# Cross network on Trainium2: the first layer as one product, its remainder rows on VectorE, and two transfers swapped

## The chip, the cores and the metric

The kernel runs on one core of one Trainium2 chip. Its time is device time in microseconds (us), the median of the runs shown. Beside it stands one profiled execution, whose own time and span are used where instructions are counted; the span is measured from the first to the last instruction, so what lies before and after it is not in it.

## The reference

Six layers of a cross network. Every layer multiplies the running activation by a square weight matrix, adds a bias, multiplies by the network's input and adds the running activation. The input is 4096 rows of 416 features, all in bf16.

```python
B, F, D, L = 4096, 26, 16, 6
Din = min(F * D, 1024)          # 416
# x0 (4096, 416), ws (6, 416, 416), bs (6, 416)
def reference(x0, ws, bs):
    x = x0
    for l in range(ws.shape[0]):
        x = x0 * (x @ ws[l] + bs[l]) + x
    return x
```

In the first layer x is x0 itself.

## The kernel before

**Layout.** Features lie on partitions. Of the 416 features, 384 make three blocks of 128 (`NK = 3`, index `m` for output blocks and `k` for input blocks) and 32 are left over, the remainder. The 4096 rows are two halves (`s = 0, 1`) of 2048, each of four column groups (`g`) of 512 columns. `XM[0]` holds the transposed x0 of the three blocks, `XM[1]` and `XM[2]` the running activation by turns; `XR[0..2]` hold the remainder, with group g of a half on partitions 32g to 32g+31. `XRx` is a copy of the first `XR` with its two partition halves exchanged.

**Loads.** The x0 blocks come in by DMA transposes, one for each column group (`load_x0t(s, g)`, line 78), all issued on SP's queue in a written order; the remainder comes as rows (`load_xrem`, line 83): half 0 in two parts (partitions 0 to 63 from ACT's queue, 64 to 127 from SP's) and half 1 in one. Behind the eight transposes SP issues the later layers' weights (`load_wm`, `load_wr`), the x0 rows for the last layer and the last bias. `x0_rem` (lines 155 to 160) turns remainder rows into `XR[0]`: a 32x32 block transpose, a reordering copy, and the copy into `XRx`. For the second part of half 0 the two copies run on GpSimd (POOL), for the others on VectorE (DVE).

**First layer.** `first_layer(s)` (line 208) fills three pairs of PSUM banks with columns groups 0 and 1 (`pa[m]`, by `full`, line 214, three matmuls for one block and group), adds the remainder's contribution (`row`, line 221), and does the same for groups 2 and 3 (`pb[m]`). PSUM has four such pairs, handed out in turn by `two_banks`, so a new block waits until ACT has emptied the pair that it takes over. `rem_first` computes the remainder's own output for both halves.

**Eviction.** `ew_main` (lines 162 to 167) empties a pair of banks: ACT adds the bias `bM` and writes bf16 into one of six buffers `t`, DVE multiplies `t` by x0 (line 166) and adds the running activation (line 167). `ew_rem` (lines 169 to 173) does this for the remainder with `bR`.

**Layers 1 to 4** go through six tiles (half s, block m) two by two: `mm_full` (line 179) and `mm_row` (line 185) for the tile, then its evictions; `rem_pair` (lines 191, 196) stands behind the first two tiles. The first tile's `mm_row` reads the remainder activation of the layer before. **The last layer** works with rows on partitions (lines 332 to 346) and writes the output.

Every engine executes its own instructions in the order in which the kernel's text issues them; the order is written out by hand, and no scheduler moves anything.

Of the kernel before, what the change touches and what calls it, by code (L numbers as in the profile page):

```python
# [10 lines left out]
ALU = mybir.AluOpType  # L11
# [5 lines left out]
def kernel(  # L17
# [7 lines left out]
    nc = tc.nc  # L25
    B, D = x0.shape
    L = ws.shape[0]
    P = 128
    NK = 3
# [4 lines left out]
    CW = 512  # L34
# [24 lines left out]
    bM = const.tile([P, NK, L], FP32)  # L59
    bR = const.tile([P, L], FP32)  # L60
# [5 lines left out]
    XRx = [big.tile([P, CW], BF16, name=f"XRx{s}") for s in range(NS)]  # L66
    XM = [big.tile([P, NK, B], BF16, name=f"XM{i}") for i in range(3)]
    XR = [big.tile([P, NS * CW], BF16, name=f"XR{i}") for i in range(3)]

    def col0(s, g):  # L70
        return SW * s + CW * g
# [4 lines left out]
    def load_x0t(s, g):  # L76
        c0 = col0(s, g)
        nc.sync.dma_start_transpose(out=XM[0][:, :, c0:c0 + CW], in_=x0[c0:c0 + CW, 0:NK * P])  # L78


    def load_xrem(eng, s, p0, p1):
        with nc.allow_non_contiguous_dma(reason="64B row segments"):
            eng.dma_start(xrem[s][p0:p1], x0[SW * s + 16 * p0:SW * s + 16 * p1, NK * P:D].rearrange("(p t) r -> p t r", t=16))  # L83
# [18 lines left out]
        nc.vector.tensor_copy(WR[32 * g:32 * g + 32, 0, :], WR[0:32, 0, :])  # L102
    load_x0t(0, 1)
    load_x0t(0, 2)
    load_xrem(nc.sync, 0, 64, 128)
    load_x0t(0, 3)
    load_x0t(1, 0)
    load_x0t(1, 1)
    load_xrem(nc.sync, 1, 0, 128)
# [21 lines left out]
    def two_banks():  # L131
        i = 2 * (turn[0] % 4)
        turn[0] += 1
        return PS[:, i:i + 2, :]

    def pe_filler(n, cols):
        for i in range(n):
            nc.tensor.matmul(PS[:, 0, 0:cols], lhsT=warm[:, 0:P], rhs=warm[:, 0:cols], start=True, stop=True, skip_group_check=True)  # L138
# [4 lines left out]
    def bias_setup():  # L143
        pb = PS[:, 7, 0:32].rearrange("p (a b) -> p a b", a=4)
        for m in range(NK):
            nc.tensor.matmul(pb[:, m, 0:L], lhsT=bsb[0:L, 128 * m:128 * m + 128], rhs=ident[0:L, 0:L], start=True, stop=True,
                             skip_group_check=True)
        for g in range(NG):
            nc.tensor.matmul(pb[32 * g:32 * g + 32, 3, 0:L], lhsT=bsb[0:L, NK * P:D], rhs=ident[0:L, 0:L], start=True, stop=True,
                             tile_position=(0, 32 * g), skip_group_check=True)  # L150
        nc.vector.tensor_copy(bM[:], pb[:, 0:NK, 0:L])
        nc.vector.tensor_copy(bR[:], pb[:, 3, 0:L])


    def x0_rem(s, p0, p1, eng):
        nc.vector.transpose(out=xrt[s][p0:p1], in_=xrem[s][p0:p1])  # L156
        eng.tensor_copy(XR[0][p0:p1, CW * s:CW * s + CW].rearrange("p (j t) -> p j t", t=16),
                              xrt[s][p0:p1].rearrange("p t j -> p j t"))
        for a in range(p0, p1, 64):
            eng.tensor_copy(XRx[s][64 - a:128 - a, :], XR[0][a:a + 64, CW * s:CW * s + CW])  # L160

    def ew_main(l, s, m, h, pt, cur, nxt):
        c0 = col0(s, 2 * h)
        t = tpool.tile([P, 2 * CW], BF16, name="t")
        nc.scalar.activation(t[:], pt.rearrange("p a b -> p (a b)"), ACT.Identity, bias=bM[:, m, l:l + 1], scale=1.0)  # L165
        nc.vector.tensor_tensor(out=t[:], in0=t[:], in1=XM[0][:, m, c0:c0 + 2 * CW], op=ALU.mult)  # L166
        nc.vector.tensor_tensor(out=nxt[:, m, c0:c0 + 2 * CW], in0=t[:], in1=cur[:, m, c0:c0 + 2 * CW], op=ALU.add)  # L167

    def ew_rem(l, s, pr, curR, nxtR):
        tr = tpool.tile([P, 2 * CW], BF16, name="t")  # L170
        nc.scalar.activation(tr[:, 0:CW], pr, ACT.Identity, bias=bR[:, l:l + 1], scale=1.0)  # L171
        nc.vector.tensor_tensor(out=tr[:, 0:CW], in0=tr[:, 0:CW], in1=XR[0][:, CW * s:CW * s + CW], op=ALU.mult)
        nc.vector.tensor_tensor(out=nxtR[:, CW * s:CW * s + CW], in0=tr[:, 0:CW], in1=curR[:, CW * s:CW * s + CW], op=ALU.add)  # L173

    def mm_full(l, s, m, g, pts, cur, first, last):
# [32 lines left out]
    def first_layer(s):  # L208
        cur, nxt = XM[0], XM[1]

        def full(pt, m, h, gl, first, last):
            c0 = col0(s, 2 * h + gl)
            for k in range(NK):
                nc.tensor.matmul(pt[:, gl, :], lhsT=WM[:, 0, k, 128 * m:128 * m + 128], rhs=cur[:, k, c0:c0 + CW],  # L214
                                 start=(first and k == 0), stop=(last and k == NK - 1), skip_group_check=True)

        def row(pt, m, h, swapped, first):
            for gl in range(2):
                r0 = 32 * ((2 * h + gl + 2 * swapped) % 4)
                src = XRx[s][r0:r0 + 32, :] if swapped else XR[0][r0:r0 + 32, CW * s:CW * s + CW]  # L220
                nc.tensor.matmul(pt[:, gl, :], lhsT=WR[r0:r0 + 32, 0, 128 * m:128 * m + 128], rhs=src,
                                 start=first, stop=(not first), tile_position=(r0, 0), skip_group_check=True)

        pa = [two_banks() for m in range(NK)]
        if s == 0:
            for gl in range(2):
                for m in range(NK):
                    full(pa[m], m, 0, gl, True, False)
        else:
            for m in range(NK):  # L230
                for gl in range(2):
                    full(pa[m], m, 0, gl, True, False)
        pb = [two_banks()]
        row(pa[0], 0, 0, 0, False)
        row(pa[1], 1, 0, 1, False)
        row(pa[2], 2, 0, 0, False)
        if s == 1:
            row(pb[0], 0, 1, 0, True)
        if s == 0:
            x0_rem(0, 64, 128, nc.gpsimd)  # L240
        for m in range(NK):
            ew_main(0, s, m, 0, pa[m], cur, nxt)
        for gl in range(2):
            full(pb[0], 0, 1, gl, s == 0, s == 1)
        if s == 1:
            ew_main(0, s, 0, 1, pb[0], cur, nxt)
        for m in range(1, NK):
            pb.append(two_banks())
            for gl in range(2):
                full(pb[m], m, 1, gl, True, False)  # L250
        if s == 0:
            row(pb[0], 0, 1, 0, False)
            row(pb[2], 2, 1, 1, False)
            row(pb[1], 1, 1, 0, False)
            x0_rem(1, 0, 128, nc.vector)
            for m in range(NK):
                ew_main(0, s, m, 1, pb[m], cur, nxt)
        else:
            row(pb[1], 1, 1, 0, False)
            row(pb[2], 2, 1, 1, False)  # L260
            rem_first(pb)

    bias_setup()
    pe_filler(1, CW)
    x0_rem(0, 0, 64, nc.vector)

    def rem_pair(l, cur, curR, nxtR, feeds_last):
        pr2 = two_banks()
        for s in range(NS):
            mm_rem(l, s, pr2[:, s, :], cur, curR)  # L270
        for s in range(NS):
            ew_rem(l, s, pr2[:, s, :], curR, nxtR)
            if feeds_last:
                nc.sync.dma_start_transpose(out=scrR[s][:], in_=nxtR[:, CW * s:CW * s + CW])
                nc.gpsimd.tensor_copy(XLrows[:, 16 * s:16 * s + 16, NK * P:D].rearrange("p (g i) r -> p i g r", g=NG),  # L275
                                      scrR[s][:].rearrange("p i (g r) -> p i g r", g=NG))

    def rem_first(pb):
        pr2 = two_banks()
        for s in range(NS):  # L280
            mm_rem(0, s, pr2[:, s, :], XM[0], XR[0])
        for s in range(NS):
            ew_rem(0, s, pr2[:, s, :], XR[0], XR[1])
            ew_main(0, 1, 1 + s, 1, pb[1 + s], XM[0], XM[1])

    first_layer(0)
    fill_wd(1, L)
    first_layer(1)
    cur, curR = XM[1], XR[1]
    for l in range(1, LL):  # L290
        nxt, nxtR = XM[1 + (l % 2)], XR[1 + (l % 2)]
# [27 lines left out]
    l = LL  # L319
# [107 lines left out]
```

## Time and profile before

| | us |
|---|---|
| median of 3 runs | 132.49 (131.76 to 132.85) |
| profiled execution, its own time | 132.9 |
| its span, first to last instruction | 131.1 |
| PE (TensorE matmul) busy | 122.8 |
| DVE busy | 111.2 |
| ACT busy | 84.0 |
| POOL busy | 8.3 |
| mean granted TensorE clock | 0.991 of full speed |

Engines work at the same time, so their busy times don't add up to the span. A row of a timeline gives the start, the duration from the first start to the last end of the merged instructions, the engine (a trailing q means the engine's queue of DMA issues), the line, the operation and the count; what stands in brackets is idle time of that engine ahead of the row and what ended it. A matmul of 512 columns has a row of 0.38 us, but one starts every 0.22 us, since matmuls are pipelined; a short stall is therefore seen in the distance between starts and not as idle time.

### The profile page before, as it was taken

How to read it: one execution, taken by the hardware profiler on the slowest of the kernel's cores; microseconds unless marked ns; L12 is line 12 of the kernel's file. 1: busy time of each engine (PE TensorE's matmuls, PEld its weight loads, DVE VectorE, ACT ScalarE, POOL GpSimd, SP SyncE). 2: the span in 40 equal slices, each digit the busy share in tenths (PEclk: the TensorE clock that was granted, in tenths of full speed). 3: DMA queues.
4: the chain of work that ended last, by engine and by line, in shares of the span. 5: the costliest groups of instructions: out<-in, count | busy, mean ns of one | idle time of the engine just before them, and what ended most of it. 6: DMA issues, size and time to landing. Idle time of an engine off the chain costs nothing.

```text
span 131.1 us, 3942 instructions
## 1 busy us (share of the span) xinstructions
PE 122.8 (94%) x1681; PEld 54.5 (42%) x1683; DVE 111.2 (85%) x196; ACT 84.0 (64%) x92; POOL 8.3 (6%) x20
## 2 busy tenths in 40 slices
PE   6996999997999999999999999999999999999950
PEld 2342343443434344544454444344544445544420
DVE  1256939999999999999898989898989999999990
ACT  1307196686939485939477948668757777567760
POOL 4105000250000000000000000000000400000000
PEclk9999999999999999999999999999999999999996
DMA  3999999999990000000000000000297899996553
GB/s 92 264 184 171 182 160 251 216 313 333 332 331 28 5 0 3 5 0 5 0 5 0 5 0 5 0 0 5 49 156 164 169 131 235 199 329 206 184 179 100
DMA packets 42021, 16.37 MB, mean 125 GB/s; under 512 B 30826, under 2 KB 42004, under 8 KB 42004
## 3 DMA queue, kind: packets, MB, share of 16 engines
q1 hardware_dynamic: 40504, 15.70, 54.5%
q10 hardware_dynamic: 1500, 0.42, 1.5%
q8 instruction: 13, 0.21, 0.7%
q14 instruction: 4, 0.03, 0.1%
HBM read 6.15 MB, written 3.41 MB: 73 GB/s over the span
## 4 chain that ended last, share of the span: by engine, by line
PE 72%; SPq 16%; DMA 5%; DVE 3%; issue 1%; ACT 0%; DVEq 0%
PE PS L179 46%; SPq L78 13%; PE PS L332 12%; PE PS L185 5%; DMA WM<-in_ws_dram 5%; PE PS L196 4%; PE PS L341 2%; SPq L86 1%; PE PS L191 1%; PE PS L346 1%; SPq L83 1%; DVE t L367 1%; SPq L74 1%; DVE o L370 1%; DVE t L166 1%
## 5 line engine op out<-in xcount | busy, mean ns | idle before, releaser
L165 ACT ACTIVATE t<-PS,bM 128x1024 bf16<-128x1024 f32 x60 | 62.2, 1115 | 32.2 <-PE PS L185 22.1
L179 PE MATMUL PS<-XM,WM 128*32 128x512 bf16 x1152 | 65.2, 379 | 0.0
L167 DVE TENSOR_TENSOR XM<-t,XM 128x1024 bf16<-128x1024 bf16 x60 | 42.2, 703 | 3.5
L166 DVE TENSOR_TENSOR t<-t,XM 128x1024 bf16<-128x1024 bf16 x60 | 42.1, 702 | 2.4 <-ACT t L165 2.4
L179 PEld LDWEIGHTS <-WM 128*32 128x32 bf16 x1152 | 29.7, 97 | 33.8 <-issue 5.1
L332 PE MATMUL PS<-WM,XM 128*128 128x416 bf16 x96 | 17.9, 340 | 0.0
L214 PE MATMUL PS<-XM,WM 128*128 128x512 bf16 x70 | 16.4, 379 | 1.4 <-DMA XM<-in_x_dram 1.2
L356 ACT CAST t<-PS 128x832 bf16<-128x832 f32 x12 | 10.2, 852 | 5.0 <-PE PS L332 2.5
L332 PEld LDWEIGHTS <-XM 128*128 128x128 bf16 x96 | 8.9, 98 | 8.7 <-issue 2.2
L214 PEld LDWEIGHTS <-WM 128*128 128x128 bf16 x72 | 6.8, 97 | 10.6 <-issue 3.2
L196 PE MATMUL PS<-XM,WM 128*32 128x512 bf16 x120 | 8.2, 379 | 0.0
L185 PE MATMUL PS<-XR,WR 32*128 32x512 bf16 x96 | 7.3, 379 | 0.7 <-DVE XR L173 0.7
L171 ACT ACTIVATE t<-PS,bR 128x512 bf16<-128x512 f32 x10 | 6.8, 695 | 1.7 <-PE PS L196 1.7
L358 DVE TENSOR_TENSOR o<-t,XLrows 128x832 bf16<-128x832 bf16 x12 | 7.1, 592 | 0.5
L357 DVE TENSOR_TENSOR t<-t,X0rows 128x832 bf16<-128x832 bf16 x12 | 7.0, 584 | 0.0
L275 POOL COPY XLrows<-scrR 128x512 bf16<-128x512 bf16 x2 | 1.4, 694 | 73.9 <-DMA scrR<-XR 73.9
L138 PE MATMUL PS<-warm 128*128 128x512 bf16 (+1 forms) x12 | 4.8, 576 | 1.2 <-DVE warm L89 1.2
L156 DVE STREAM_TRANSPOSE xrt<-xrem 64x512 bf16<-64x512 bf16 (+1 forms) x3 | 2.1, 708 | 3.8 <-DMA xrem<-in_x_dram 3.8
L173 DVE TENSOR_TENSOR XR<-t,XR 128x512 bf16<-128x512 bf16 x10 | 4.2, 425 | 0.8
L366 ACT CAST t<-PS 128x416 bf16<-128x416 f32 x8 | 4.0, 506 | 1.0 <-PE PS L332 0.8
L196 PEld LDWEIGHTS <-WM 128*32 128x32 bf16 x120 | 3.2, 97 | 3.2
L102 DVE COPY WR<-WR 32x416 bf16<-32x416 bf16 x3 | 0.8, 260 | 4.4 <-DMA WR<-in_ws_dram 4.3
(37 smaller groups left out, 40.7 us busy)
## 6 DMA issues: line engine op xcount, KB each, us to landing
X0rows<-in_x_dram SPq DMA_DIRECT2D x4, 832.0 KB, 10.0
out_dram<-o SPq DMA_DIRECT2D x12, 208.0 KB, 2.3
WM<-in_ws_dram SPq DMA_DIRECT2D x5, 312.0 KB
out_dram<-o SPq DMA_DIRECT2D x8, 104.0 KB, 1.8
WR<-in_ws_dram SPq DMA_DIRECT2D x4, 130.0 KB, 5.4
WM<-in_ws_dram ACTq DMA_DIRECT2D x1, 312.0 KB, 3.2
XM<-in_x_dram SPq DMA_TRANSPOSE x8, 4.8
xrem<-in_x_dram SPq DMA_DIRECT2D x1, 128.0 KB
```

What stands on the lines that cost most here:

```text
L78: nc.sync.dma_start_transpose(out=XM[0][:, :, c0:c0 + CW], in_=x0[c0:c0 + CW, 0:NK * P])
L165: nc.scalar.activation(t[:], pt.rearrange("p a b -> p (a b)"), ACT.Identity, bias=bM[:, m, l:l + 1], scale=1.0)
L166: nc.vector.tensor_tensor(out=t[:], in0=t[:], in1=XM[0][:, m, c0:c0 + 2 * CW], op=ALU.mult)
L167: nc.vector.tensor_tensor(out=nxt[:, m, c0:c0 + 2 * CW], in0=t[:], in1=cur[:, m, c0:c0 + 2 * CW], op=ALU.add)
L179: nc.tensor.matmul(pts[g // 2][32 * q:32 * q + 32, g % 2, :], lhsT=WM[:, l, k, 128 * m + 32 * q:128 * m + 32 * q + 32], rhs=cur[:, k, c0:c ...
L185: nc.tensor.matmul(pts[g // 2][:, g % 2, :], lhsT=WR[32 * g:32 * g + 32, l, 128 * m:128 * m + 128], rhs=curR[32 * g:32 * g + 32, CW * s:CW ...
L196: nc.tensor.matmul(pr[32 * g:32 * g + 32, :], lhsT=WM[:, l, k, NK * P:D], rhs=cur[:, k, c0:c0 + CW], start=False, stop=(k == NK - 1), tile ...
L214: nc.tensor.matmul(pt[:, gl, :], lhsT=WM[:, 0, k, 128 * m:128 * m + 128], rhs=cur[:, k, c0:c0 + CW], start=(first and k == 0), stop=(last ...
L332: nc.tensor.matmul(py[g // 2][:, g % 2, 0:D], lhsT=cur[:, k, q_cols(q, g)], rhs=WM[:, l, k, :], start=(first and k == 0), stop=((not first ...
L356: nc.scalar.copy(tv, py[h][:, :, 0:D])
L357: nc.vector.tensor_tensor(out=tv, in0=tv, in1=X0rows[:, b0:b0 + 5:4, :], op=ALU.mult)
L358: nc.vector.tensor_tensor(out=o[:], in0=tv, in1=XLrows[:, b0:b0 + 5:4, :], op=ALU.add)
```

## The change

It has four parts. The first layer's bias columns of `bM` and `bR` are stored with 1 added, and for layer 0 `ew_main` and `ew_rem` write the product of `t` and x0 straight into the next activation and return, without the add. The fourth column group's transpose of half 0 is issued ahead of the remainder's second part. The two copies of that part move from POOL to DVE. In half 1 the first blocks come in the order (m, group) (0,0), (1,0), (0,1), (1,1), (2,0), (2,1), and in half 0 the remainder rows of `pb` come in the order 0, 1, 2.

```diff
     load_x0t(0, 2)
+    load_x0t(0, 3)
     load_xrem(nc.sync, 0, 64, 128)
-    load_x0t(0, 3)
     load_x0t(1, 0)
...
-        nc.vector.tensor_copy(bM[:], pb[:, 0:NK, 0:L])
-        nc.vector.tensor_copy(bR[:], pb[:, 3, 0:L])
+        nc.vector.tensor_scalar(out=bM[:, :, 0:1], in0=pb[:, 0:NK, 0:1], scalar1=1.0, scalar2=None, op0=ALU.add)
+        nc.vector.tensor_scalar(out=bR[:, 0:1], in0=pb[:, 3, 0:1], scalar1=1.0, scalar2=None, op0=ALU.add)
+        nc.vector.tensor_copy(bM[:, :, 1:L], pb[:, 0:NK, 1:L])
+        nc.vector.tensor_copy(bR[:, 1:L], pb[:, 3, 1:L])
...
-    def x0_rem(s, p0, p1, eng):
+    def x0_rem(s, p0, p1):
...
-        eng.tensor_copy(XR[0][p0:p1, ...
+        nc.vector.tensor_copy(XR[0][p0:p1, ...
...
-            eng.tensor_copy(XRx[s][64 - a:128 - a, :], ...
+            nc.vector.tensor_copy(XRx[s][64 - a:128 - a, :], ...
...  # ew_main
-        nc.vector.tensor_tensor(out=t[:], in0=t[:], in1=XM[0][:, m, c0:c0 + 2 * CW], op=ALU.mult)
+        x0c = XM[0][:, m, c0:c0 + 2 * CW]
+        if l == 0:
+            nc.vector.tensor_tensor(out=nxt[:, m, c0:c0 + 2 * CW], in0=t[:], in1=x0c, op=ALU.mult)
+            return
+        nc.vector.tensor_tensor(out=t[:], in0=t[:], in1=x0c, op=ALU.mult)
         nc.vector.tensor_tensor(out=nxt[:, m, c0:c0 + 2 * CW], in0=t[:], in1=cur[:, m, c0:c0 + 2 * CW], op=ALU.add)
...  # ew_rem in the same way, with XR[0] and nxtR
...  # first_layer, half 1
-            for m in range(NK):
-                for gl in range(2):
-                    full(pa[m], m, 0, gl, True, False)
+            for m, gl in ((0, 0), (1, 0), (0, 1), (1, 1), (2, 0), (2, 1)):
+                full(pa[m], m, 0, gl, True, False)
...
-            x0_rem(0, 64, 128, nc.gpsimd)
+            x0_rem(0, 64, 128)
...  # first_layer, half 0
             row(pb[0], 0, 1, 0, False)
+            row(pb[1], 1, 1, 0, False)
             row(pb[2], 2, 1, 1, False)
-            row(pb[1], 1, 1, 0, False)
```

More of the change, by code (lines that the diff above doesn't have):

```diff
@@ L150, in bias_setup @@
                              tile_position=(0, 32 * g), skip_group_check=True)
-        nc.vector.tensor_copy(bM[:], pb[:, 0:NK, 0:L])
-        nc.vector.tensor_copy(bR[:], pb[:, 3, 0:L])
-    def x0_rem(s, p0, p1, eng):
+        nc.vector.tensor_scalar(out=bM[:, :, 0:1], in0=pb[:, 0:NK, 0:1], scalar1=1.0, scalar2=None, op0=ALU.add)
[3 more added lines that the diff above has]
+    def x0_rem(s, p0, p1):
         nc.vector.transpose(out=xrt[s][p0:p1], in_=xrem[s][p0:p1])
-        eng.tensor_copy(XR[0][p0:p1, CW * s:CW * s + CW].rearrange("p (j t) -> p j t", t=16),
+        nc.vector.tensor_copy(XR[0][p0:p1, CW * s:CW * s + CW].rearrange("p (j t) -> p j t", t=16),
                               xrt[s][p0:p1].rearrange("p t j -> p j t"))
         for a in range(p0, p1, 64):
-            eng.tensor_copy(XRx[s][64 - a:128 - a, :], XR[0][a:a + 64, CW * s:CW * s + CW])
+            nc.vector.tensor_copy(XRx[s][64 - a:128 - a, :], XR[0][a:a + 64, CW * s:CW * s + CW])
     def ew_main(l, s, m, h, pt, cur, nxt):
@@ L171, in ew_rem @@
         nc.scalar.activation(tr[:, 0:CW], pr, ACT.Identity, bias=bR[:, l:l + 1], scale=1.0)
-        nc.vector.tensor_tensor(out=tr[:, 0:CW], in0=tr[:, 0:CW], in1=XR[0][:, CW * s:CW * s + CW], op=ALU.mult)
+        x0c = XR[0][:, CW * s:CW * s + CW]
+        if l == 0:
+            nc.vector.tensor_tensor(out=nxtR[:, CW * s:CW * s + CW], in0=tr[:, 0:CW], in1=x0c, op=ALU.mult)
+            return
+        nc.vector.tensor_tensor(out=tr[:, 0:CW], in0=tr[:, 0:CW], in1=x0c, op=ALU.mult)
         nc.vector.tensor_tensor(out=nxtR[:, CW * s:CW * s + CW], in0=tr[:, 0:CW], in1=curR[:, CW * s:CW * s + CW], op=ALU.add)
@@ L252, in first_layer @@
             row(pb[0], 0, 1, 0, False)
+            row(pb[1], 1, 1, 0, False)
             row(pb[2], 2, 1, 1, False)
-            row(pb[1], 1, 1, 0, False)
-            x0_rem(1, 0, 128, nc.vector)
+            x0_rem(1, 0, 128)
             for m in range(NK):
@@ L264 @@
     pe_filler(1, CW)
-    x0_rem(0, 0, 64, nc.vector)
+    x0_rem(0, 0, 64)
     def rem_pair(l, cur, curR, nxtR, feeds_last):
```

## The prediction

> **What bounds the kernel now.** I read the page's first lines, then PE's waits, then the timelines of PE, SP, DVE, POOL and ACT up to 35 us, last the stages.
>
> ```profile
> span 131.1 us, 3942 instructions
> PE 122.8 (94%) x1681; PEld 54.5 (42%) x1683; DVE 111.2 (85%) x196; ACT 84.0 (64%) x92; POOL 8.3 (6%) x20
> PE PS L214 <- DMA XM<-in_x_dram: 1.2, 1, 1.2
> PE PS L185 <- DVE XR L173: 0.7, 1, 0.7
> 30.84:50.08 19.24, 19.24 (x344) 8.57 (x345) 18.69 (x32) 13.61 (x14) 0.00 (x0) 1.00 0.51 152
> 50.08:69.32 19.24, 19.24 (x349) 8.70 (x347) 17.69 (x30) 13.61 (x14) 0.00 (x0) 1.00 0.01 3
> ```
>
> The last two rows give each engine's busy time in a stage, PE first. From 30.84 us on PE has no gap: two layers take 19.24 us each, all of it PE, at a granted clock of 1.00. DVE fills 18.69 us of the first and 17.69 of the second, the first still carrying a backlog. PE's two waits longer than a matmul's latency, between the warm-up and layer 5, are 1.2 us on a DMA transpose and 0.7 us on DVE. The change takes no matmul away, so it can gain only where PE stalls ahead of 31 us.
>
> ```profile
> 10.59 0.82 PE L214 MATMUL PS<-XM,WM 128*128 128x512 bf16 x3
> 12.61 3.40 PE L214 MATMUL PS<-XM,WM 128*128 128x512 bf16 x14 [1.20 <-DMA XM<-in_x_dram]
> 15.94 0.39 PE L221 MATMUL PS<-XR,WR 32*128 32x512 bf16 x2
> 16.48 4.06 PE L214 MATMUL PS<-XM,WM 128*128 128x512 bf16 x18
> 20.47 0.39 PE L221 MATMUL PS<-XR,WR 32*128 32x512 bf16 x2
> 21.24 0.59 PE L214 MATMUL PS<-XM,WM 128*128 128x512 bf16 x2
> 21.45 0.88 PE L214 MATMUL PS<-XM,WM 128*128 128x512 bf16 x2
> 21.96 0.81 PE L214 MATMUL PS<-XM,WM 128*128 128x512 bf16 x3
> 27.35 2.76 PE L179 MATMUL PS<-XM,WM 128*32 128x512 bf16 x48
> 30.84 0.61 PE L185 MATMUL PS<-XR,WR 32*128 32x512 bf16 x8 [0.73 <-DVE XR L173]
> 35.71 2.76 PE L179 MATMUL PS<-XM,WM 128*32 128x512 bf16 x48
> 38.41 0.61 PE L185 MATMUL PS<-XR,WR 32*128 32x512 bf16 x8
> 17.14 1.96 SPq L78 DMA_TRANSPOSE XM<-in_x_dram  x1
> DMA to landing us min/median/max: 4.7/4.8/5.4
> ```
>
> Matmuls of this form start 0.22 us apart (21.24 to 21.45), but after 21.45 the next starts at 21.96: a third stall, of 0.29 us, too short for the list of waits. It stands where half 1's block `pb[0]` turns to its second group, which needs the last x0 transpose. SP issued that one at 17.14; with the median 4.8 us to landing it arrives at 21.9. So this **gate** at 21.96 is set by the load queue: whatever PE saves before it is lost again in front of it.
>
> **The change, part by part.**
>
> *Transposes and remainder swapped.*
>
> ```profile
> 6.50 0.67 SPq L83 DMA_DIRECT2D xrem<-in_x_dram  x1
> 7.22 2.71 SPq L78 DMA_TRANSPOSE XM<-in_x_dram  x1
> 13.63 0.59 SPq L83 DMA_DIRECT2D xrem<-in_x_dram  x1
> ```
>
> The fourth group's issue moves from 7.22 to 6.50, so its data should come 0.72 us earlier, and PE resumes near 11.9 instead of 12.61. The remainder's second part is issued when that transpose's issue is over: 6.50 + 2.71 + 0.04 = 9.25 instead of 6.50. Nothing else on SP's queue moves: the two issues together take what they took, so the last transpose is still issued near 17.14 and the gate stays at 21.96. Value of the 0.72 us: nothing, it is spent at the gate.
>
> *Copies from POOL to DVE, and what now waits at the head of DVE's queue.*
>
> ```profile
> 7.64 0.70 DVE L156 STREAM_TRANSPOSE xrt<-xrem 64x512 bf16<-64x512 bf16 x1 [0.77 <-DMA xrem<-in_x_dram]
> 8.38 0.59 DVE L157 COPY XR<-xrt 64x512 bf16<-64x512 bf16 x1
> 9.00 0.28 DVE L160 COPY XRx<-XR 64x512 bf16<-64x512 bf16 x1
> 10.37 0.71 DVE L156 STREAM_TRANSPOSE xrt<-xrem 64x512 bf16<-64x512 bf16 x1 [1.09 <-DMA xrem<-in_x_dram]
> 11.63 1.16 DVE L166 TENSOR_TENSOR t<-t,XM 128x1024 bf16<-128x1024 bf16 x1 [0.55 <-ACT t L165]
> 18.44 0.71 DVE L156 STREAM_TRANSPOSE xrt<-xrem 128x512 bf16<-128x512 bf16 x1 [1.97 <-DMA xrem<-in_x_dram]
> 19.82 0.61 DVE L160 COPY XRx<-XR 64x512 bf16<-64x512 bf16 x2
> 16.37 3.13 ACT L165 ACTIVATE t<-PS,bM 128x1024 bf16<-128x1024 f32 x3 [2.76 <-PE PS L221]
> ```
>
> The second part came 3.87 us after its issue (6.50 to 10.37), half 1's remainder 4.81 us after (13.63 to 18.44). From 9.25 that gives 13.1 to 14.1; I take 13.1, the same transfer's own row. On DVE the chain of transpose and two copies takes 1.33 us to `XR` and 1.64 us to `XRx` (7.64 to 8.97 and 9.28): ready at 14.4 and 14.7, at the late end 15.4 and 15.7. PE's rows of `pb`, now at 15.94, come at 11.9 + 3.33 = 15.2, the swapped ones last. So PE waits between nothing and 0.2 us there. The remainder's transpose, waiting for its DMA until 13.1, holds DVE's whole queue: the three first products, which began at 11.63, begin at 14.7. ACT waits for none of them, having six buffers, and PE reads their results only at 27.35.
>
> *Half 1's order.* Block (1,0) takes over the bank pair of `pb[0]` of half 0, which ACT empties from 0.43 us after its rows (15.94 to 16.37), for 1.1 us: until 16.75. PE would reach it at 15.2 + 0.54 + 0.66 = 16.4 and waits 0.35 us; the old order would come there 0.66 us later. The half's 3.99 us (16.48 to 20.47) then end at 20.1, and half 1's `XRx`, which hangs on the unmoved DMA of 18.44, is whole at 20.43. With 0.27 us for the rows behind it and 0.66 us for a group PE stands at the gate near 21.4. These waits, 0.35 us and whatever is above, are covered by the 0.55 us that remain; without that cover they would cost their full length.
>
> *Bias + 1.* Two small DVE instructions more. The one that stores `bM` from PSUM now takes 0.18 us; I take that for each, 0.36 us in all, bounds nothing and twice that. DVE then idles 0.77 us for the remainder's DMA (the row at 7.64), which hides them; without it they would delay `XR`, and PE reads that at 10.06.
>
> ```profile
> 6.62 0.18 DVE L151 COPY bM<-PS 128x18 f32<-128x18 f32 x1
> ```
>
> *One product, no sum: the part that pays.*
>
> ```profile
> 26.72 0.69 ACT L171 ACTIVATE t<-PS,bR 128x512 bf16<-128x512 f32 x1 [1.69 <-PE PS L196]
> 28.87 1.12 ACT L165 ACTIVATE t<-PS,bM 128x1024 bf16<-128x1024 f32 x1
> 29.91 0.42 DVE L172 TENSOR_TENSOR t<-t,XR 128x512 bf16<-128x512 bf16 x1
> 30.36 0.42 DVE L173 TENSOR_TENSOR XR<-t,XR 128x512 bf16<-128x512 bf16 x1
> L167 DVE TENSOR_TENSOR XM<-t,XM 128x1024 bf16<-128x1024 bf16 x60 | 42.2, 703 | 3.5
> ```
>
> Twelve sums of 0.70 us and two of 0.42 us leave DVE: 9.3 us. The copies from POOL bring back 0.9. Now the remainder's `t` of half 0 is ready at 27.41 but waits for DVE until 29.91, and its sum ends at 30.78; PE's rows follow at 30.84. With the backlog gone, DVE does one product from 27.45 to 27.87. What is late next: `mm_row` of the second tile takes over the pair of `pb[2]`, which ACT empties until 29.99 (28.87 + 1.12). PE's own work in front needs 2.70 us, the distance in a later layer (35.71 to 38.41): 27.35 + 2.70 = 30.05. So the rows start at 30.05 instead of 30.84: **0.79 us** gained, bounds 0.6 (a handover that costs 0.2) and 0.79. Nothing after that hangs on DVE's lead, so all of it moves up to the end.
>
> Sum: 132.9 - 0.79 = 132.1 for the profiled execution, whose span of 131.1 has 1.8 us around it. That execution is 0.4 us above the median; from 132.49 the sum gives 131.7.
>
> **The rivals.**
>
> *The gate opens earlier.* DMA engines are not evenly busy (stage, then busy times; the last two columns are DMA's share and GB/s):
>
> ```profile
> 10.00:11.00 1.00, 1.00 (x9) 0.32 (x9) 0.63 (x1) 0.51 (x1) 0.00 (x0) 1.00 1.11 243
> 11.00:12.00 1.00, 0.41 (x2) 0.10 (x1) 0.45 (x2) 1.00 (x2) 0.79 (x1) 1.00 0.51 75
> ```
>
> At 11 us there is a hole of 0.6 us of share, behind the remainder's small runs. If the new order closes it, all later transfers land up to 0.54 us earlier (0.60 / 1.11), and PE, by its own chain at 21.4, can use it: -0.54 - 0.79 gives 131.2, with a smaller 30.05 stage or more holes closed 130.6. Against it: the same transfers, only in another order, stay in the queue. The Trainium skill (DMA: Bandwidth & Descriptors, Latency and other measured facts) gives DMA transposes 261 GB/s; 0.39 MB would take an estimated 1.5 us, and the issues shown take 1.96 and 2.71 us, so by this page there is room for this rival.
>
> *Another wait takes the place at 30 us.* ACT's 29.99 leaves only 0.06 us ahead of 30.05. If ACT's chain from 26.72 stretches by 0.7 us, `mm_row` waits for the bank and not for `XR`: 132.4. For it: ACT has no gap there. Against it: ACT waits for PE at its head (1.69 us), not for DVE.
>
> *The remainder lands late, and PE waits for it.* Its place is the head of DVE's queue and the rows of `pb`. Call its landing T: rows at T + 1.33, the gate reached 6.2 us after the rows as above, so it decides from T = 14.4 on, one us for one. T = 17, if it must stand behind the next two transposes as well (13.1 and twice the 1.96 us of an issue), costs 2.6 us: 132.49 - 0.79 + 2.6 = 134.3. Against it: both known remainders came within 4.81 us, that is by 14.1. The Trainium skill (TensorE: Matmul & The Clock Gate, Part 1) has the clock halved after an idle window of about 3.4 us, which would make this worse by an estimated 1.7 us; the 1.2 us wait of this trace left it at 1.00, and no longer one is seen.
>
> **How the numbers follow.** Forecast, only the 0.79: 0.48. Gate earlier: 0.32. Another wait at 30 us: 0.10. Late remainder: 0.10. The time is the forecast's, 131.7. Its own range is 131.2 to 132.3, from the spread of the three runs. The whole reaches to 130.6 for the gate and to 133.0 past the exchanged wait; only the late remainder and some tails stay out. One per cent, 1.3 us or 131.2, is about what a measurement of this kernel can tell from no change. Below it lie a quarter of the forecast (0.12) and two thirds of the gate (0.22): 0.34. Above 133.8 lies the late remainder, 0.10. Within stay 0.56.
>
> **What would show it.** Right: no wait of PE on `XR` near 30 us, the first rows of layer 1 some 2.7 us after its first matmul, DVE idle between evictions before 31 us, PE's wait at 11 to 12 us shorter but a longer stall ahead of 21.96, and everything behind it shifted by the same amount. The first step is wrong if the gate moves from 21.96 by over 0.3 us; the third if ACT or a bank ends the wait at 30 us; the second if PE waits for `XR` or `XRx` at 15 us. The forecast as a whole is wrong if PE's work from 31 us on changes its length.

## The result, and the profile after

The changed kernel takes 131.34 us (median of 20 runs, 130.84 to 132.15), the kernel before 132.03 us (20 runs, 131.62 to 132.85). The ratio is 0.9946, 95% interval 0.9929 to 0.9963: 0.7 us faster, 0.5 to 0.9. The profiled execution took 131.1 us with a span of 129.3, 1.8 us less than the profiled execution before; that one was the slowest of its 20 runs, so the pair of profiles shows more than twice what the medians show.

The page's busy times, then PE's waits behind the warm-up:

```profile
span 129.3 us, 3927 instructions
PE 122.5 (95%) x1681; PEld 54.4 (42%) x1683; DVE 103.1 (80%) x186; ACT 83.9 (65%) x92; POOL 5.4 (4%) x18
PE PS L225 <- DMA XM<-in_x_dram: 0.4, 1, 0.4
PE PS L225 <- ACT t L168: 0.2, 1, 0.2
```

DVE has 8.1 us less work and POOL 2.9; PE has the same. The wait on DVE's `XR` is gone, and a wait of 0.24 us on ACT, for the bank pair of block (1,0), is new. In the timelines (lines moved: 214 is now 225, 221 is 232, 179 is 190, 185 is 196, 165 is 168):

```profile
10.70 4.21 PE L225 MATMUL PS<-XM,WM 128*128 128x512 bf16 x17
14.84 0.39 PE L232 MATMUL PS<-XR,WR 32*128 32x512 bf16 x2
16.44 3.40 PE L225 MATMUL PS<-XM,WM 128*128 128x512 bf16 x15 [0.24 <-ACT t L168]
20.31 4.06 PE L225 MATMUL PS<-XM,WM 128*128 128x512 bf16 x17
26.36 2.76 PE L190 MATMUL PS<-XM,WM 128*32 128x512 bf16 x48
29.06 0.61 PE L196 MATMUL PS<-XR,WR 32*128 32x512 bf16 x8
11.92 0.71 DVE L158 STREAM_TRANSPOSE xrt<-xrem 64x512 bf16<-64x512 bf16 x1 [2.41 <-DMA xrem<-in_x_dram]
13.29 0.29 DVE L162 COPY XRx<-XR 64x512 bf16<-64x512 bf16 x1
17.31 0.71 DVE L158 STREAM_TRANSPOSE xrt<-xrem 128x512 bf16<-128x512 bf16 x1 [1.80 <-DMA xrem<-in_x_dram]
26.45 0.42 DVE L181 TENSOR_TENSOR XR<-t,XR 128x512 bf16<-128x512 bf16 x1 [1.39 <-ACT t L178]
27.88 1.12 ACT L168 ACTIVATE t<-PS,bM 128x1024 bf16<-128x1024 f32 x1
8.46 0.68 SPq L83 DMA_DIRECT2D xrem<-in_x_dram  x1
```

From layer 1's first matmul to its first rows PE now needs 29.06 - 26.36 = 2.70 us; before it was 30.84 - 27.35 = 3.49. That is the 0.79 us of the prediction, to the hundredth. The other 0.99 us of the two profiles lie ahead of it: block `pb[0]` of half 1 starts at 20.31 and goes through without a stall, so its second group began at about 20.97 instead of 21.96. The experiments had to say whether the swap did that.

### The profile page after: what moved, and what is told of

It reads as the page before. It is cut to its first block, busy times and chain, and to the rows that moved or that the text cites. A ratio compares the mean times of both kernels' runs of the same rounds, so it can differ in the third digit from the quotient of the medians.

```text
span 129.3 us, 3927 instructions
## 1 busy us (share of the span) xinstructions
PE 122.5 (95%) x1681; PEld 54.4 (42%) x1683; DVE 103.1 (80%) x186; ACT 83.9 (65%) x92; POOL 5.4 (4%) x18
## 4 chain that ended last, share of the span: by engine, by line
PE 88%; DMA 5%; DVE 1%; ACT 1%; SPq 1%; issue 1%; DVEq 0%
PE PS L190 49%; PE PS L342 12%; PE PS L225 10%; PE PS L196 5%; PE PS L207 5%; DMA XM<-in_x_dram 5%; PE PS L202 2%; PE PS L351 2%; PE PS L232 1%; PE PS L356 1%; SPq L78 1%; DVE t L377 1%; ACT t L168 1%; DVE o L380 1%; ACT t L376 0%
## 5 line engine op out<-in xcount | busy, mean ns | idle before, releaser
L173 DVE TENSOR_TENSOR t<-t,XM 128x1024 bf16<-128x1024 bf16 x48 | 33.3, 694 | 4.2 <-ACT t L168 4.2
L174 DVE TENSOR_TENSOR XM<-t,XM 128x1024 bf16<-128x1024 bf16 x48 | 33.5, 699 | 3.1
L171 DVE TENSOR_TENSOR XM<-t,XM 128x1024 bf16<-128x1024 bf16 x12 | 7.9, 689 | 2.3 <-ACT t L168 2.1
```

The costliest lines, as they stand in the source:

```text
L173: nc.vector.tensor_tensor(out=t[:], in0=t[:], in1=x0c, op=ALU.mult)
```

## The experiments

All ratios are against the kernel before, run beside each kernel; intervals in brackets. The last column is, in each kernel's single profile, the time from layer 1's first matmul to its first rows.

| run | what it is | ratio | first matmul to rows, us |
|---|---|---|---|
| e1 | before, again | 0.9996 (0.9976 to 1.0015) | 27.10 to 30.57: 3.47 |
| e2 | before + one product | 0.9967 (0.9947 to 0.9987) | 27.08 to 29.77: 2.69 |
| e3 | changed, sums back | 1.0005 (0.9990 to 1.0021) | 26.75 to 30.45: 3.70 |
| e4 | before + swap | 1.0029 (1.0011 to 1.0047) | 26.64 to 30.67: 4.03 |
| e5 | changed, no swap | 0.9929 (0.9907 to 0.9951) | 27.02 to 29.72: 2.70 |
| e6 | changed, old block order | 0.9951 (0.9927 to 0.9974) | 27.57 to 30.26: 2.69 |
| e7 | changed, remainder later | 1.0200 (1.0155 to 1.0244) | 31.19 to 33.89: 2.70 |
| e8 | changed, one more small load | none | 33.10 to 35.80: 2.70 |
| e9 | before + product in first three | 0.9977 (0.9957 to 0.9997) | 26.61 to 29.77: 3.16 |
| e10 | before + product in later three | 0.9956 (0.9933 to 0.9978) | 27.89 to 30.59: 2.70 |
| e11 | changed, remainder loads on ACT's queue at once | 0.9990 (0.9975 to 1.0006) | 27.29 to 29.98: 2.69 |
| e12 | the same, behind ACT's first activation | 1.0012 (0.9988 to 1.0036) | 27.49 to 30.19: 2.70 |

### Which part carries the gain: e1 to e4

e1, no edit.

> The kernel before, unchanged, against itself. Theory W (the gain is the wait near 30 us that leaves) and theory Q (the gain is the load queue that runs earlier because two transfers are swapped) both expect a ratio of 1.000 within 0.002. Its profile is a second look at where the last x0 transpose lets PE go on in half 1's first block of groups 2 and 3: 21.96 us in the first look. If that place moves by 0.5 us or more between two profiles of one kernel, a single pair of profiles cannot tell W from Q.

The ratio is 0.9996, and PE went on with `pb[0]`'s second group near 21.71 (21.05 and three matmuls), 0.25 us earlier than in the first profile of the kernel before, half of the 0.5 us that the expectation named. Layer 1's first matmul stands at 27.10 against 27.35. So this place moves from run to run; how far, the later profiles show.

e2, the product without the rest:

```diff
 # the kernel before, with bias + 1 in column 0 of bM and bR, and in ew_main (ew_rem alike)
+        if l == 0:
+            nc.vector.tensor_tensor(out=nxt[:, m, c0:c0 + 2 * CW], in0=t[:], in1=x0c, op=ALU.mult)
+            return
```

> The kernel before with bias + 1 and one product in layer 0; transfers, POOL copies and block order stay as before. W: nearly the whole gain, 0.994 to 0.996, rows of layer 1 2.7 us after its first matmul instead of 3.5. Q: at most a third of the gain, 0.998 or above.

0.9967, 0.4 us: between what W and Q expected and nearer to W; its interval overlaps the changed kernel's. The rows of layer 1 follow after 2.69 us. But the list of waits names a new limit, the last x0 transpose. Reckoned from the starts, as the prediction did, the stall is 21.68 - 20.43 - 3 * 0.22 = 0.59 us, where the first profile of the kernel before had 0.29 us and e1 none:

```profile
20.43 0.82 PE L224 MATMUL PS<-XM,WM 128*128 128x512 bf16 x3
21.68 3.40 PE L224 MATMUL PS<-XM,WM 128*128 128x512 bf16 x14 [0.44 <-DMA XM<-in_x_dram]
```

e3, the rest without the product:

```diff
 # the changed kernel, bias columns as before
-        if l == 0:
-            nc.vector.tensor_tensor(out=nxt[:, m, c0:c0 + 2 * CW], in0=t[:], in1=x0c, op=ALU.mult)
-            return
```

> The changed kernel with layer 0's sums and the plain bias put back; swap, copies on DVE and block order stay changed. W: no gain, 0.999 to 1.002, and the wait for XR in front of layer 1's first rows is back with 0.7 us or more. Q: 0.996 or below, since the queue is the changed one.

1.0005: no gain, and the wait is back with 0.93 us. PE started layer 1 at 26.75, 0.35 us earlier than in e1, but its rows came only 0.12 us earlier, at 30.45: most of the lead was lost in front of `XR`:

```profile
26.75 2.76 PE L182 MATMUL PS<-XM,WM 128*32 128x512 bf16 x48
30.45 0.61 PE L188 MATMUL PS<-XR,WR 32*128 32x512 bf16 x8 [0.93 <-DVE XR L176]
```

e4, the swap alone:

```diff
     load_x0t(0, 2)
+    load_x0t(0, 3)
     load_xrem(nc.sync, 0, 64, 128)
-    load_x0t(0, 3)
```

> The kernel before with only the two transfers swapped. W: 0.999 to 1.002; PE's wait at 11 to 12 us shrinks by about 0.7 us and comes back later. Q: 0.996, with PE going on near 21.4 instead of 21.96 in half 1's first block of groups 2 and 3.

1.0029, a little slower, where both expected no loss. PE reached layer 1 at 26.64, earlier still, and waited 1.27 us for `XR`: whatever came earlier on PE went into that wait. DVE shows where a loss can come from: its first three products and sums, held back by the later remainder, now run right up to half 1's remainder, which has no idle time in front of it. Two of them are long, 1.42 and 1.09 us, while POOL makes its two copies (13.15 to 15.67); in e3, where DVE makes these copies, all six take 0.69 us or less:

```profile
12.31 0.71 DVE L156 STREAM_TRANSPOSE xrt<-xrem 64x512 bf16<-64x512 bf16 x1 [2.62 <-DMA xrem<-in_x_dram]
13.78 1.42 DVE L167 TENSOR_TENSOR XM<-t,XM 128x1024 bf16<-128x1024 bf16 x1
15.12 1.09 DVE L166 TENSOR_TENSOR t<-t,XM 128x1024 bf16<-128x1024 bf16 x1
18.19 0.70 DVE L156 STREAM_TRANSPOSE xrt<-xrem 128x512 bf16<-128x512 bf16 x1
30.67 0.61 PE L185 MATMUL PS<-XR,WR 32*128 32x512 bf16 x8 [1.27 <-DVE XR L173]
```

These four settle the larger question: without the product nothing is gained, with it alone 0.4 us (0.2 to 0.7) is, of 0.7 (0.5 to 0.9).

### What the wait near 30 us really hung on: e9, e10

Putting the rows with sums side by side: from the start of half 1's remainder transpose on DVE to layer 1's first rows it is 18.44 to 30.84 in the kernel before, 18.07 to 30.57 in e1, 17.89 to 30.45 in e3, 18.19 to 30.67 in e4: 12.4 to 12.6 us each time, wherever PE stood. That is DVE working without a break. In the kernel before and in e1 the stretch starts with the landing of half 1's remainder (1.97 and 1.29 us of idle time ahead of it). In e3 and e4 DVE is not idle there, and its unbroken work goes back to the landing of half 0's second part, at 12.21 and 12.31. Two kernels take three sums away each, on either side of that landing:

```diff
 # the kernel before; b1 is the first bias column + 1, all else keeps the plain bias and the sum
+        early = l == 0 and s == 0 and h == 0      # e9; in e10: s == 1 and h == 0
+        bias = b1[:, m:m + 1] if early else bM[:, m, l:l + 1]
...
+        if early:
+            nc.vector.tensor_tensor(out=nxt[:, m, c0:c0 + 2 * CW], in0=t[:], in1=x0c, op=ALU.mult)
+            return
```

> The kernel before; one product instead of product and sum in three of layer 0's evictions only: half 0, groups 0 and 1, which DVE does before half 1's remainder lands near 18 us. Theory D (what counted was DVE working without a break from that landing to the remainder's XR near 30.8 us): no gain, 0.999 to 1.002, the wait for XR in front of layer 1's first rows stays at 0.7 us. Rival T (every sum saved counts alike): the same small gain as in the other run of three sums, about a fifth of that of the product alone.

> The same with three other evictions: half 1, groups 0 and 1, which DVE does after that landing. Three sums off the unbroken stretch are about 1.9 us, more than the 0.7 us wait. D: the wait near 30 us is gone and the time is that of the product in all evictions, 0.994 to 0.997. T: 0.998 to 1.000, like the first three.

e9, DVE's start of the stretch, its end, PE's rows and the wait; then the rows of e10:

```profile
17.29 0.71 DVE L158 STREAM_TRANSPOSE xrt<-xrem 128x512 bf16<-128x512 bf16 x1 [3.10 <-DMA xrem<-in_x_dram]
29.29 0.43 DVE L182 TENSOR_TENSOR XR<-t,XR 128x512 bf16<-128x512 bf16 x1
29.77 0.61 PE L194 MATMUL PS<-XR,WR 32*128 32x512 bf16 x8 [0.40 <-DVE XR L182]
```

```profile
22.50 3.40 PE L223 MATMUL PS<-XM,WM 128*128 128x512 bf16 x14 [0.82 <-DMA XM<-in_x_dram]
28.04 0.43 DVE L181 TENSOR_TENSOR t<-t,XR 128x512 bf16<-128x512 bf16 x1 [0.83 <-ACT t L179]
30.59 0.61 PE L194 MATMUL PS<-XR,WR 32*128 32x512 bf16 x8
```

In e9 the stretch is as long as ever, 17.29 to 29.77, 12.48 us: three saved sums ahead of the landing only lengthened DVE's idle time there to 3.10 us, and PE still waited for `XR`, 0.40 us where 0.7 was expected. In e10 DVE even idles before the remainder's product, PE waits for nothing at its rows, and the time is that of the product everywhere with three sums of fourteen. So the profiles bear out D. The times alone don't separate it from T: e9 gained 0.3 us (0.0 to 0.6) where D expected nothing, and its interval overlaps that of e10. What gave e9 its part is not settled; its remainder landed 0.8 us earlier than in e1, in one profile.

### The other parts: e5, e6

e5 and e6 undo one edit each in the changed kernel (no run undoes the copies on DVE, or the order of the remainder rows, alone):

```diff
 # e5
+    load_xrem(nc.sync, 0, 64, 128)
     load_x0t(0, 3)
-    load_xrem(nc.sync, 0, 64, 128)
 # e6
-            for m, gl in ((0, 0), (1, 0), (0, 1), (1, 1), (2, 0), (2, 1)):
+            for m, gl in ((0, 0), (0, 1), (1, 0), (1, 1), (2, 0), (2, 1)):
```

> The changed kernel with the two transfers in their old order; product, copies on DVE and block order stay changed. Theory S (with the sums gone the load queue sets the end of layer 0, and the swap lets the last x0 transpose land earlier): the part of the gain that the product alone did not bring is lost, 0.996 to 0.998, with PE held in half 1's first block of groups 2 and 3 until 21.5 or later. Theory C (that part comes from the copies on DVE and the block order): 0.994 to 0.995.

> The changed kernel with half 1's first blocks in the old order. S: no difference to the changed kernel, 0.994 to 0.996; PE's short wait for ACT's bank near 16.4 us disappears or shrinks. C: 0.997 or above.

Without the swap the ratio is 0.9929, with the old block order 0.9951; neither can be told from the changed kernel's 0.9946, though e5 lies even below what C expected. S is wrong as far as it goes on the swap: the order of those two transfers is worth nothing that these runs resolve. Whether C is right, and the copies on DVE bring what the product alone did not, stays open, since e2's interval overlaps all of these. In e6 the wait on ACT is gone, as expected, and a wait of 0.71 us for the last transpose stands in its place (PE went on at 22.18). Over the ten profiles whose loads stand in one of the two orders, e1 to e6, e9, e10 and the first pair, that group starts between 20.97 (swapped) and 22.50 (e10, not swapped), and e6 at 22.18 is swapped. The 0.99 us by which the first pair of profiles differed there is within this spread. SP's queue spreads likewise: its issue of the last transpose ends at 18.03, 18.51, 18.58 and 19.17 in the four swapped profiles (the changed kernel, e4, e3, e6) and between 18.62 and 19.47 in the six others. So the queue may run a little earlier with the swap; the times show no gain from it.

### What a late remainder costs, and how tight the load queue is: e7, e8

```diff
 # e7: the changed kernel
     load_x0t(0, 3)
-    load_xrem(nc.sync, 0, 64, 128)
     load_x0t(1, 0)
     load_x0t(1, 1)
+    load_xrem(nc.sync, 0, 64, 128)
     load_xrem(nc.sync, 1, 0, 128)
```

> The changed kernel with the remainder's second part issued two transposes later still, behind the sixth. It tests the price of the prediction's slower rival. Landing near 15 us instead of 11.5, XR 1.4 us later, so PE should wait at its rows of half 0's second part until 16.4 instead of 14.8: by one us for one 1.5 us more than the changed kernel, 1.005 to 1.007. If the load queue's end covers it (S): at most 0.5 us more, 0.994 to 0.998.

The miss is large: 1.0200. The remainder landed not near 15 but at 16.7, issued behind six transposes, and the rows of half 0 waited for it. Then the clock fell. The wait and the block behind it, and the stages (TensorE's granted clock stands third from the end):

```profile
16.69 0.71 DVE L158 STREAM_TRANSPOSE xrt<-xrem 64x512 bf16<-64x512 bf16 x1 [7.43 <-DMA xrem<-in_x_dram]
18.07 0.61 PE L232 MATMUL PS<-XR,WR 32*128 32x512 bf16 x4 [3.14 <-DVE XR L159]
18.71 5.95 PE L225 MATMUL PS<-XM,WM 128*128 128x512 bf16 x18
14.90:18.00 3.10, 0.03 (x1) 0.05 (x1) 1.28 (x2) 0.00 (x0) 0.00 (x0) 1.00 0.98 125
19.00:20.00 1.00, 0.88 (x4) 0.24 (x3) 1.00 (x3) 1.00 (x2) 0.00 (x0) 0.77 0.99 158
20.00:21.00 1.00, 1.00 (x4) 0.41 (x3) 0.97 (x3) 1.00 (x2) 0.00 (x0) 0.50 1.24 302
21.00:22.00 1.00, 1.00 (x4) 0.35 (x3) 0.94 (x3) 0.62 (x1) 0.00 (x0) 0.50 1.11 283
22.00:23.00 1.00, 1.00 (x4) 0.31 (x3) 0.97 (x3) 0.00 (x0) 0.00 (x0) 0.53 1.17 223
23.00:24.00 1.00, 1.00 (x6) 0.48 (x5) 1.00 (x2) 0.00 (x0) 0.55 (x1) 1.00 1.16 210
```

PE was idle for 3.14 us; about 1.5 us after it had gone on, TensorE's clock fell to half for 3.4 us (0.77 from 19 to 20 us is half speed from about 19.5 on, 0.53 from 22 to 23 is half speed until about 22.9), and 18 matmuls took 5.95 us instead of 4.06 (the first block at 16.48 in the kernel before). Its six runs agree: at mean clocks of 0.978 to 0.987 four of them took 135.5 to 136.0 us, at 0.99 and 1.00 two took 134.1 and 134.6. The changed kernel's ratio, 0.9946, would be 131.9 us beside this kernel before (132.61): the two lost 2.2 and 2.7 us, the four 3.6 to 4.1.

```diff
 # e8: the changed kernel; scr is a tile that nobody reads
     load_xrem(nc.sync, 1, 0, 128)
+    load_scr()          # x0 rows 0 to 2047, the 32 remainder columns, 64-byte runs
     load_x0t(1, 2)
```

> The changed kernel with one more load of half 0's remainder rows (128 partitions, runs of 64 bytes, into a tile that nobody reads) on SP's queue right ahead of the last two x0 transposes. S: these land 0.6 to 1.5 us later and PE is held by the same amount, 0.999 to 1.006. If the queue's end does not bind: 0.994 to 0.996.

No ratio is given: five of its six runs took 136.9 to 137.9 us at mean clocks of 0.974 to 0.985, the sixth 134.75 us at 0.998. The profile is one of the five.

```profile
14.81 2.10 SPq L89 DMA_DIRECT2D scr<-in_x_dram  x1
22.24 0.81 PE L232 MATMUL PS<-XM,WM 128*128 128x512 bf16 x3 [1.49 <-DMA XM<-in_x_dram]
25.15 1.86 PE L232 MATMUL PS<-XM,WM 128*128 128x512 bf16 x4 [2.10 <-DMA XM<-in_x_dram]
24.00:25.00 1.00, 0.00 (x0) 0.00 (x0) 0.42 (x1) 0.00 (x0) 0.00 (x0) 0.50 1.12 294
```

One more small load held PE for 1.49 and 2.10 us: the last group began at 25.15 instead of 20.97, 4.2 us for a load of 0.13 MB, more than the 1.5 us that S allowed. The run at 0.998 took 2.9 us more than the 131.9 us reckoned for the changed kernel, so the 4.2 us of this one profile are not the price in every run. The load queue in front of that group has little slack, which is S's other half, and here it is borne out. The last row is the clock: TensorE stood at half speed there too, after these two waits with three matmuls between them.

### Small loads off SP's queue: e11, e12

```diff
 # e11: the changed kernel, neither load on SP's queue
     load_xrem(nc.scalar, 0, 0, 64)
+    load_xrem(nc.scalar, 0, 64, 128)
+    load_xrem(nc.scalar, 1, 0, 128)
 # e12: the same two lines behind nc.scalar.activation(dz...) instead
```

> The changed kernel with both remaining remainder loads issued from ACT's queue at its start instead of SP's. Theory S (SP's queue with its loads in order sets when PE can end layer 0): the last two x0 transposes are issued 1.2 us earlier and PE ends layer 0 up to 1 us earlier, 0.988 to 0.993. Rival B (the DMA engines' throughput sets it, whichever queue issues): the transposes land as before and the early ones later, 0.994 to 1.000.

> The changed kernel with the two remaining remainder loads issued from ACT's queue behind its first small activation, near 4.5 us and after, so that the first two x0 transposes keep the DMA engines to themselves. If the load from ACT's queue at the start only failed because it held back the early transposes (second transpose used at 8.70 instead of 8.13 us, third group's rows later): PE reaches half 1's groups 2 and 3 without waits, up to 0.6 us earlier than the changed kernel, 0.990 to 0.994. If any load beside the transposes holds back the one that PE needs next (throughput is what is short): 0.994 to 1.000.

0.9990 and 1.0012: the gain is gone in both. SP finished its eight transposes 0.7 us earlier (17.3 instead of 18.0), the remainders were there in time, and no wait stands at the last group. But the early transposes, which the small loads now run beside, came later:

```profile
8.74 2.10 PE L225 MATMUL PS<-XM,WM 128*128 128x512 bf16 x9 [0.95 <-DMA XM<-in_x_dram]
12.64 3.40 PE L225 MATMUL PS<-XM,WM 128*128 128x512 bf16 x15 [0.50 <-DMA XM<-in_x_dram]
21.44 4.06 PE L225 MATMUL PS<-XM,WM 128*128 128x512 bf16 x18
```

These rows of e12 show PE going on at 8.74 instead of 8.13 with the second transpose, at 12.64 instead of 11.51 with the fourth, and reaching the last block at 21.44 instead of 20.31. For the fourth transpose this stands out from the spread: SP issued it at 6.47 in e11 and 6.61 in e12, and its group started at 12.43 and 12.64; in the six profiles with the swapped order and the small loads on SP's queue (the changed kernel, e3, e4, e6, e7, e8) it was issued between 6.39 and 6.77, and its group started between 11.35 and 11.91. The Trainium skill (DMA: Bandwidth & Descriptors, Issuing engines are not separate DMA queues) says that loads issued by several engines run on the same 16 DMA engines and save issue time only; this trace agrees, with 0.7 us of issue time saved and 1.1 us lost on PE, each from one pair of profiles. No kernel of this study is clearly better than the changed one: its 0.9946 lies inside e5's interval.

## Why the prediction was right, point by point

**The product without the sum.** Right in mechanism and size in the profile: DVE's wait went, the next bound at that place was ACT's eviction of `pb[2]`, which ends at 27.88 + 1.12 = 29.00, 0.06 us ahead of the rows, and 2.70 us were needed. In time the product alone gave 0.4 us (0.2 to 0.7, e2), less than 0.79. The step that was too simple is that the gate stands at 21.96. In e1 the last transpose landed in time and PE did not stall there, and still waited 0.7 us for `XR`; the limit of the kernel before was DVE's stretch of 12.4 us from the remainder's landing, not the gate. Once it is gone, the gate, or PE's own way to it, is the limit, and how far ahead of the end of DVE's stretch that lies changes from run to run: the stall at the gate was 0.29 us in the first profile, none in e1 and 0.59 us in e2.

**"The gate stays at 21.96", and the swap is worth nothing.** The value is right: e4 and e5 show no gain from the swap. The place is not: 20.97 in the profile after, by more than the 0.3 us that the prediction had named as its own refutation. So the rival in which the queue runs earlier seemed borne out by the pair of profiles, by 0.99 us, and is not borne out by the runs that were made for it; the earliest start, 20.97, and the second latest, 22.18, are both of the swapped order.

**Remainder's second part at the head of DVE's queue.** Right in that PE did not wait. The terms were pessimistic: SP issued it at 8.46 instead of 9.25, since the transpose ahead took 1.82 us and not 2.71, DVE began at 11.92 instead of 13.1, and `XRx` was whole at 13.58, 1.3 us ahead of PE's rows at 14.84.

**Half 1's block order.** The bank wait came as reckoned, 0.24 us against 0.35. That the order itself buys nothing measurable is e6.

**Bias + 1.** Hidden, as forecast; DVE then still idled before the remainder.

**The slower rival.** Its mechanism is real and its rule, rows 1.33 us after DVE starts, holds in e7 (16.69 to 18.07, 1.38). Its landing behind two more transposes, 17, came at 16.7. Its price without the clock, 2.3 us for a landing at 16.7, fits the two runs at mean clocks of 0.99 and 1.00, which lost 2.2 and 2.7 us; by the ratios of all runs the loss is 3.4 (1.0200 against 0.9946). By the half clock after an idle window that the Trainium skill gives (TensorE: Matmul & The Clock Gate, Part 1), for which the prediction had estimated 1.7 us, it would be 4.0. The trace agrees with the halving, with 1.89 us in one block, and the other four runs with the sum, 3.6 to 4.1; but the idle time here, 3.14 us, is shorter than the Trainium skill's 3.4, and two of the six runs show no such loss.

**The sum.** 131.7 was forecast from the median of three runs, 0.8 us less than it; measured is 0.7 less (0.5 to 0.9), and 131.34 because the 20 runs of before lie 0.46 us below the three. That the whole comes so near to 0.79 is in part luck: the prediction gave all of it to the product, which alone brought 0.4 (0.2 to 0.7), and no run shows which other part brought the rest, or whether there is a rest.

## What to carry to other kernels

Where a wait names a late engine, follow that engine back to where it last stood idle: what ended that idle time is what really bounds the place, and only work behind it pays when it is removed (three sums behind it did what fourteen did, three ahead of it left a wait of 0.40 us). Where a load queue and an engine's backlog end within a microsecond of each other, taking away the one gives only the distance to the other, which changes from run to run, and a single pair of profiles can overstate it by more than a factor of two. Take a second profile of the kernel before ahead of any story on where time went.

## What the runs showed that was not expected

A wait of 3.14 us was enough to halve TensorE's clock for 3.4 us in the profile of e7, and four of its six runs show a mean clock lowered to match, which turns one late load into a loss half as large again. DVE's products and sums of 128x1024 took 0.98 to 1.42 us while POOL made its two copies (the kernel before, e1, e4), and 0.69 at that place in e3, where DVE makes them. A load of 0.13 MB in runs of 64 bytes put PE's last group back by 4.2 us when issued in front of the last two transposes (e8, one profile); a transpose of 0.39 MB held SP's queue for 2.71 us in the kernel before, and SP's issue of the small load itself took 2.10.
